# A conformer block with recorded instruction order: the limits that choose the order, from 18 phases to 49 segments

## The chip, the cores and the metric

The kernel runs on one core of a Trainium2 chip. The metric is the device time of one execution in microseconds (us); most executions of one kernel agree within 0.3%. Each run also lists the mean clock that TensorE was granted (1.00 is full speed). Engines are named as in the profile: PE is TensorE (PEld its weight loads), ACT is ScalarE, DVE is VectorE, POOL is GpSimd, SP is SyncE.

## The reference

A conformer block in bf16: B = 2 sequences of T = 4000 rows, D = 144, K = 5 taps, H = 4 heads of 36.

```python
x = x + 0.5 * (silu(layernorm(x) @ w_ff1a) @ w_ff1b)
q, k, v = heads(layernorm(x) @ w_qkv)                     # 4 heads of 36
x = x + (softmax(q @ k.T * 36**-0.5) @ v) @ w_o
a, b = split(layernorm(x) @ w_pw1)
h = a * sigmoid(b)
x = x + silu(depthwise_conv(h, dw, taps=5)) @ w_pw2
x = x + 0.5 * (silu(layernorm(x) @ w_ff2a) @ w_ff2b)
return layernorm(x)
```

The large part is attention: 2 x 4 x 4000 x 4000 exponentials.

## The kernel before

The queries are cut into 16 chunks of 500 (8 for each sequence), the keys into 63 key tiles of 64 (the last is short). One *tile* of work is 64 keys by one query chunk by 4 heads: 1008 tiles in all. A tile's scores are four 64-row matrix products into two banks of PSUM (the memory that takes TensorE's results). Then its exponentials are made either by ScalarE (one instruction over two neighbouring banks, 1000 columns) or by VectorE (seven instructions over two single banks, an approximation). Then TensorE multiplies them by the values. Everything else (feed-forward, projections, gated convolution, norms) is "background" that runs beside the attention. Six banks serve scores and background alike.

No engine decides anything at run time. While the program is built, every instruction goes through a recorder that keeps a planned clock for each engine, and the order in which they are recorded is the order in which each engine executes:

```python
def op(self, eng, name, *a, r=(), w=(), q=None, cost=0.1, kind=None, lat=None, **k):
    ...
    start = ready = self.free[eng]
    for d, raw in o.deps:
        if d.eng != eng or d.q is not None or (raw and eng != "pe"):
            ready = max(ready, d.done + self.SEM[eng])
    ...
    if eng == "pe":
        if kind != self.kind:
            start += self.SWITCH          # planned cost of another tiling mode
        self.kind = kind
    self.free[eng] = o.t1 = start + cost
```

What comes next is chosen among candidates by planned start, under limits that depend on how far attention is (`now("NAME")`). MAXQ, for one, is how many score tiles may wait for ScalarE, LIVE how many VectorE tiles may be under way, AHEAD how early ScalarE's next scores must be planned:

```python
BASE = dict(AHEAD=0.56, DSLACK=0.4, DGAP=4.0, OFREE=1, OBATCH=1, LATE=0.3, BMIN=1.6, SOON=2, LIVE=3, MAXQ=3, EARLY=2)
POLICY = {                                # one value for each of 18 phases
    "DSLACK": [0.4, 0.4, 1.5, 1.5, 1.5, 1.5, 1.5, 0.6, 1.0, ...],
    "LIVE": [3, 2, 2, 2, 3, 3, 3, 3, 3, 2, 2, 3, 3, 3, 2, 3, 3, 3],
    ...
}
def now(k):
    return POLICY[k][its[min(n_s[0], NIT - 1)][0]] if k in POLICY else BASE[k]

# in pick_any: S = scores of a tile, O = value products, T = background
near = [q for q in pe if q[0] <= pemin + PW]
deadline = act_end() - now("AHEAD")       # ScalarE must have its next scores by then
if ts is not None:
    limit = max(deadline, ts) + (now("LATE") if lag() else 0.0)
ok = [q for q in bg if max(q[0], R.free["pe"]) + q[2].req.dur + ... <= limit]
...
if ok:
    return min(ok, key=lambda q: not q[2].req.hold)      # background that fits
if s:
    return s[0]                                          # else scores
if o:
    return o[0]

def due():                                # give the next tile to VectorE?
    if n >= NIT or not DVE_EXP or live_dve[0] >= now("LIVE") or early[0] >= now("EARLY") or lag():
        return False
    return (... and R.free["dve"] < R.free["pe"] + now("DSLACK") and R.free["pe"] > last_dve[0] + now("DGAP"))
```

A ScalarE tile needs a free *pair* of banks, a VectorE tile and most background one bank at a time:

```python
def emit_S(n):
    ...
    lo, hi = banks.take_pair()            # two neighbouring banks
    scores(n, 0, lo, 0.0525)
    scores(n, 1, hi, 0.0525)
```

The softmax here doesn't subtract the row's maximum and nothing guards it: scores larger than these inputs give would overflow.

## Time and profile before

| | before |
|---|---|
| time, median of 3 runs | 938.69 us (938.61 to 938.76) |
| span of the profile, clock | 937.0 us, 0.999 |
| ScalarE busy | 893.2 us (95%), so 43.8 us idle |
| VectorE busy | 864.1 us (92%) |
| TensorE busy | 891.4 us (95%) |
| ScalarE idle: until the first exponential / to the end of the first gap / to the copy that follows the last exponential / from there on | 9.5 / 5.4 / 16.3 / 12.6 us |

Three engines stand at 92 to 95%, so busy shares alone do not name the bound. All recorded instructions carry one source line (L169, the recorder's), so groups are told apart by the names of their tiles: QT,KT is a score product, PT,VA a value product, XT,WA and WB,HT feed-forward, WQKV a value projection, PT<-PS on ScalarE an exponential, TH a tanh.

### The profile page before, as it was taken

How to read it: one execution, taken by the hardware profiler on the slowest of the kernel's cores; microseconds unless marked ns; L12 is line 12 of the kernel's file. 1: busy time of each engine (PE TensorE's matmuls, PEld its weight loads, DVE VectorE, ACT ScalarE, POOL GpSimd, SP SyncE). 2: the span in 40 equal slices, each digit the busy share in tenths (PEclk: the TensorE clock that was granted, in tenths of full speed). 3: DMA queues.
4: the chain of work that ended last, by engine and by line, in shares of the span. 5: the costliest groups of instructions: out<-in, count | busy, mean ns of one | idle time of the engine just before them, and what ended most of it. 6: DMA issues, size and time to landing. Idle time of an engine off the chain costs nothing.

```text
span 937.0 us, 26616 instructions
## 1 busy us (share of the span) xinstructions
PE 891.4 (95%) x11427; PEld 405.4 (43%) x11427; DVE 864.1 (92%) x1905; ACT 893.2 (95%) x1141; POOL 291.9 (31%) x518
## 2 busy tenths in 40 slices
PE   8999999999999999999999999999999999999996
PEld 7543434343444443344434343334344343434456
DVE  7998898999999799998989999998999899998796
ACT  5799999999999999998999999999999999999985
POOL 4120152232240551324404236203334313424233
PEclk9999999999999999999999999999999999999999
DMA  4000000000000000000000000000000000000000
GB/s 117 27 2 2 1 2 1 1 2 2 2 1 1 3 2 1 2 2 8 2 2 8 1 14 3 1 1 14 1 2 8 8 2 9 8 2 8 1 8 26
DMA packets 7319, 7.30 MB, mean 8 GB/s; under 512 B 2376, under 2 KB 7202, under 8 KB 7202
## 3 DMA queue, kind: packets, MB, share of 16 engines
q1 hardware_dynamic: 5788, 5.00, 1.8%
q8 instruction: 89, 1.46, 0.7%
q10 hardware_dynamic: 1414, 0.62, 0.3%
q14 instruction: 28, 0.23, 0.1%
HBM read 3.31 MB, written 2.30 MB: 6 GB/s over the span
## 4 chain that ended last, share of the span: by engine, by line
ACT 50%; PE 32%; DVE 14%; POOL 2%; issue 1%; DMA 0%; POOLq 0%; DVEq 0%
ACT PT L169 44%; PE PS L169 32%; DVE PT L169 8%; ACT TH L169 5%; DVE ST L169 1%; DVE HT L169 1%; POOL XN L169 1%; DVE X L169 1%; POOL RS L169 1%; DVE XT L169 1%; DVE OTF L169 1%; DMA X<-in_x_dram 0%; DVE AN L169 0%; DVE KT L169 0%; DVE XN L169 0%
## 5 line engine op out<-in xcount | busy, mean ns | idle before, releaser
L169 ACT ACTIVATE PT<-PS 128x1000 bf16<-128x1000 f32 (+1 forms) x867 | 801.7, 1046 | 13.8 <-PE PS L169 12.4
L169 PE MATMUL PS<-QT,KT 64*64 64x500 bf16 x3968 | 412.9, 384 | 27.4 <-ACT PT L169 21.6
L169 PE MATMUL PS<-PT,VA 64*37 64x500 bf16 x3968 | 361.6, 375 | 2.9 <-DVE OTF L169 1.4
L169 PEld LDWEIGHTS PS<-QT,KT 64*64 64x64 bf16 x3968 | 125.0, 104 | 225.4 <-ACT PT L169 142.4
L169 DVE TENSOR_SCALAR PT<-PS 128x500 uint16<-128x500 f32 x282 | 188.8, 671 | 11.9 <-PE PS L169 11.2
L169 DVE TENSOR_TENSOR PT<-PT 128x1000 uint16<-128x1000 uint16 (+1 forms) x282 | 190.1, 679 | 1.7
L169 POOL TENSOR_SCALAR RS<-ST 125x4 f32<-125x4 f32 x112 | 37.3, 333 | 460.2 <-DVE ST L169 455.1
L169 DVE TENSOR_SCALAR PT<-PT 128x1000 uint16<-128x1000 uint16 (+1 forms) x423 | 169.9, 418 | 2.3
L169 PEld LDWEIGHTS PS<-PT,VA 64*37 64x37 bf16 x3968 | 114.9, 95 | 113.0 <-issue 32.7
L169 POOL TENSOR_SCALAR XN<-X,RS 125x144 bf16<-125x144 bf16 x224 | 135.3, 616 | 5.8
L169 POOL TENSOR_TENSOR RS<-RS,NHALF 125x4 f32<-125x4 f32 (+2 forms) x101 | 97.8, 973 | 100.8 <-DVE RS L169 96.1
L169 ACT ACTIVATE TH<-PS 128x500 bf16<-128x500 f32 (+2 forms) x203 | 108.7, 558 | 7.1 <-PE PS L169 6.4
L169 DVE SCALAR_TENSOR_TENSOR HT<-TH,PS 128x500 bf16<-128x500 bf16 (+1 forms) x140 | 83.8, 615 | 9.7 <-ACT TH L169 9.2
L169 PE MATMUL PS<-XT,WA 72*128 72x500 bf16 (+2 forms) x280 | 73.9, 360 | 0.6 <-DVE VA L169 0.3
L169 DVE SCALAR_TENSOR_TENSOR X<-PS,X 125x288 bf16<-125x288 f32 (+1 forms) x128 | 57.2, 452 | 11.5 <-PE PS L169 9.6
L169 DVE BATCH_NORM_STATS2 ST<-X 125x6 f32<-125x288 bf16 x160 | 65.6, 447 | 1.4 <-DMA X<-in_x_dram 1.3
L169 PE MATMUL PS<-WB,HT 128*125 128x144 bf16 (+1 forms) x640 | 52.2, 230 | 1.5 <-ACT HT L169 1.1
L169 PEld LDWEIGHTS PS<-WB,HT 128*125 128x125 bf16 (+1 forms) x640 | 44.2, 136 | 15.6 <-issue 7.0
L169 PE MATMUL PS<-IDENT,XN 125*72 125x125 bf16 x512 | 42.4, 221 | 3.1 <-POOL XN L169 1.6
L169 DVE COPY XT<-PS 72x1000 bf16<-72x1000 bf16 (+1 forms) x64 | 39.6, 619 | 4.9 <-PE PS L169 4.3
L169 POOL COPY U<-U 128x2 bf16<-128x2 bf16 (+1 forms) x54 | 18.5, 368 | 73.8 <-DVE U L169 73.8
L169 PEld LDWEIGHTS PS<-IDENT,XN 125*72 125x72 bf16 x512 | 31.4, 112 | 22.1 <-issue 10.5
(88 smaller groups left out, 602.3 us busy)
## 6 DMA issues: line engine op xcount, KB each, us to landing
X<-in_x_dram SPq DMA_DIRECT2D x16, 140.6 KB
out_dram<-XN SPq DMA_DIRECT2D x14, 140.6 KB
WA<-in_w_ff1a_dram ACTq DMA_DIRECT2D x1, 144.0 KB
WB<-in_w_ff1b_dram ACTq DMA_DIRECT2D x1, 144.0 KB, 2.7
WA<-in_w_ff2a_dram SPq DMA_DIRECT2D x1, 144.0 KB
WB<-in_w_ff2b_dram SPq DMA_DIRECT2D x1, 144.0 KB
out_dram<-XN SPq DMA_DIRECT2D x2, 70.3 KB
WQKV<-in_w_qkv_dram ACTq DMA_DIRECT2D x1, 121.5 KB
```

Of the source, the lines that this page charges most:

```text
L169: ins = getattr(eng, o.name)(*o.a, **o.k)
```

## The change

Nothing is computed otherwise. A beam search over the limits, judged by the planned idle time of ScalarE and VectorE, gave a new table with a set of values for every 21 tiles. Three limits that were constants (PW, TWIN, BGPICK) come into the table, BGPICK with its old value 0 throughout, and AHEAD is tabled too. The core of the diff (twelve more lists of 49 values cut):

```diff
-    BASE = dict(AHEAD=0.56, DSLACK=0.4, DGAP=4.0, OFREE=1, OBATCH=1, LATE=0.3, BMIN=1.6, SOON=2, LIVE=3, MAXQ=3, EARLY=2)
+    SEG = 21
     POLICY = {
-        "LIVE": [3, 2, 2, 2, 3, 3, 3, 3, 3, 2, 2, 3, 3, 3, 2, 3, 3, 3],
-        "MAXQ": [3, 3, 3, 3, 3, 3, 3, 3, 2, 2, 2, 2, 2, 3, 3, 3, 3, 3],
         ...
+        "LIVE": (
+            3, 3, 2, 2, 1, 3, 3, 2, 3, 2, 3, 3, 3, 3, 3, 3,
+            2, 3, 3, 3, 3, 1, 1, 2, 2, 2, 2, 2, 2, 2, 1, 3,
+            3, 3, 3, 3, 3, 3, 2, 3, 3, 3, 3, 3, 3, 3, 3, 3,
+            3,
+        ),
+        "MAXQ": (
+            1, 1, 3, 3, 1, 3, 3, 3, 3, 3, 3, 3, 2, 2, 1, 3,
+            3, 3, 2, 2, 2, 1, 1, 2, 2, 2, 2, 2, 1, 1, 2, 2,
+            2, 2, 3, 3, 3, 2, 2, 3, 3, 3, 1, 3, 2, 2, 3, 3,
+            3,
+        ),
         ...
     }
-    BGPICK = 0
-    TWIN = 0.1
@@
     def now(k):
-        return POLICY[k][its[min(n_s[0], NIT - 1)][0]] if k in POLICY else BASE[k]
+        return POLICY[k][seg[0]]
+    seg = [0]
@@
-    PW = 0.12
-        near = [q for q in pe if q[0] <= pemin + PW]
+        near = [q for q in pe if q[0] <= pemin + now("PW")]
@@
     while n_s[0] < NIT or eq or pend or live_dve[0]:
+        seg[0] = max(seg[0], n_s[0] // SEG)
```

## The prediction

> **What bounds the kernel now.** I read the page's head first, then busy time by stretch, then the timelines of ScalarE and TensorE where ScalarE stood still. The head leaves three engines as candidates:
>
> ```profile
> span 937.0 us, 26616 instructions
> ...
> PE 891.4 (95%) x11427; PEld 405.4 (43%) x11427; DVE 864.1 (92%) x1905; ACT 893.2 (95%) x1141; POOL 291.9 (31%) x518
> ...
> ACT PT L169 44%; PE PS L169 32%; DVE PT L169 8%; ACT TH L169 5%; DVE ST L169 1%; DVE HT L169 1%; POOL XN L169 1%; DVE X L169 1%; POOL RS L169 1%; DVE XT L169 1%; DVE OTF L169 1%; DMA X<-in_x_dram 0%; DVE AN L169 0%; DVE KT L169 0%; DVE XN L169 0%
> ```
>
> The last line is the chain that ended last: half of it is ScalarE's exponentials (PT) and tanh (TH), a third TensorE. Then busy time by stretch, cut where ScalarE starts its first exponential (20.6), stops (29.3), resumes (47.6) and does the last one (905.6). After the length come busy us of PE, PEld, DVE, ACT and POOL:
>
> ```profile
> 0.00:20.60 20.60, 18.47 (x241) 16.20 (x241) 15.72 (x61) 11.08 (x23) 10.55 (x27) 1.00 0.44 116
> 20.60:29.30 8.70, 8.14 (x80) 3.16 (x77) 8.44 (x27) 8.63 (x12) 2.73 (x4) 1.00 0.32 111
> 29.30:47.60 18.30, 17.75 (x190) 10.98 (x189) 16.76 (x41) 12.96 (x28) 2.06 (x3) 1.00 0.01 2
> 47.60:450.00 402.40, 388.86 (x5110) 169.05 (x5106) 373.95 (x818) 389.74 (x477) 118.51 (x212) 1.00 0.01 2
> 450.00:850.00 400.00, 380.72 (x4864) 161.23 (x4860) 379.07 (x785) 398.19 (x494) 128.60 (x221) 1.00 0.02 5
> 850.00:905.60 55.60, 53.63 (x652) 23.20 (x649) 46.83 (x99) 53.81 (x71) 19.27 (x34) 1.00 0.01 4
> 905.60:937.00 31.40, 23.82 (x314) 21.55 (x312) 23.30 (x81) 18.84 (x41) 10.22 (x17) 0.97 0.08 24
> ```
>
> ScalarE's idle time by stretch (length less busy) is 9.5, 0.1, 5.3, 12.7, 1.8, 1.8 and 12.6 us, 43.8 in all. From 450 to 850 it is 99.5% busy: there ScalarE alone is the bound. What an order can win lies before 450, in the first gap and in the two ends. The waits say that ScalarE stands for TensorE's results, not for buffers:
>
> ```profile
> ACT PT L169 <- PE PS L169: 12.4, 20, 2.5
> ACT TH L169 <- PE PS L169: 6.4, 8, 1.3
> ```
>
> The largest such hole, first ScalarE's timeline, then TensorE's:
>
> ```profile
> 427.28 2.38 ACT L169 ACTIVATE PT<-PS 128x1000 bf16<-128x1000 f32 x3
> 431.00 0.27 ACT L169 ACTIVATE TH<-PS 80x125 bf16<-80x125 f32 x1 [1.34 <-PE PS L169]
> ...
> 428.52 0.40 PE L169 MATMUL PS<-QT,KT 64*64 64x500 bf16 x2
> ...
> 431.66 0.84 PE L169 MATMUL PS<-WB,HT 128*125 128x144 bf16 x10
> 432.43 0.71 PE L169 MATMUL PS<-WQKV,XTQ 72*64 72x72 bf16 x32
> 433.07 0.40 PE L169 MATMUL PS<-PT,VA 64*37 64x500 bf16 x4
> 433.29 0.59 PE L169 MATMUL PS<-QT,KT 64*64 64x500 bf16 x8
> ```
>
> TensorE is busy all along, but with feed-forward and projection work: from 428 to 433.29 its score products (QT,KT) come two at a time, which are VectorE's tiles; four in a row into two neighbouring banks are ScalarE's. The work is there; its order starves ScalarE.
>
> **What the Trainium skill says.** "Perfetto Trace Analysis", section "Optimization Strategy", advises to look for the gaps on the engine one optimizes and for the instruction that ends each; the reading above does that. "ScalarE: Activation LUTs", section "What ACT_TABLE_LOAD costs", gives 186 ns + 0.833 ns per element for an ACTIVATE with immediate operands and 93 ns of overlap between neighbours: 926 ns for 1000 elements. The trace is a little better: 15 exponentials from 410.99 last 13.86 us, so (13.86 - 1.05)/14 = 0.915 with a short wait inside, and undisturbed runs (4.48 us for 5 in the chain) give 0.893. "TensorEngine Tiling (Array Packing)", section "Key Properties", says that changing the tiling mode drains TensorE. The trace agrees: after four 64-row products the next 64-row group starts 0.21 to 0.23 us later, a full-array group 0.31 to 0.33, so a change costs about 0.1.
>
> **The change, part by part.** Nothing is computed otherwise. The limits by which the recorder picks the next instruction now change every 21 key tiles (49 sets) instead of by 18 phases. I built both and compared each engine's order.
>
> *Work.* Of 1008 attention tiles ScalarE does 855 + 16 short ones (before 851 + 16), VectorE 137 (141). A VectorE tile costs, by the starts of successive rows, 2 x 0.59 from PSUM + 3 x 0.33 + 2 x 0.59 = 3.35 us, so VectorE loses 13.4 us of work; ScalarE gains 4 x 0.893 = 3.6. The tail (after the last exponential) takes over some post-attention feed-forward: 4 tanh of 500 columns (0.48 each) and one of 250 (0.26) fewer, 4 Silu of 500 (0.43) and 2 of 250 (0.26) more. With a few copies and normalizations fewer (-1.7 together) ScalarE's sum is 3.6 - 2.2 + 2.2 - 1.7 = +1.9 us: 895.1 busy. TensorE's products are the same but for warm-up fillers (177 to 155) and halves in the tail; its tiling changes between first and last score rise from 1084 to 1103, 19 x 0.1 = 1.9 us on an engine with slack.
>
> *Order, steady part.* I walked TensorE's order in both, pricing each product by the trace (64-row 0.0525, 500 columns 0.21, 144 columns 0.0625, tiling change 0.1), and took the distance between successive ScalarE score tiles. Both walks are 754 us from first to last score, so TensorE is not relieved. But a distance beyond two exponentials (1.8 us) is a likely hole, and these fall from 18 to 15, their excess from 12.9 to 7.2 us; beyond 2.1 us from 8.7 to 3.7. The longest, 6.2 us, is the hole shown above; after, the longest is 4.0 there. Before 16.3 us of idle was seen from 47.6 to 905.6, against 12.9 of excess: the measure is of the right size. Scaling by 7.2/12.9 gives 9.1; I keep 9.8, since some holes are VectorE's or GpSimd's. **-6.5 us.**
>
> *Order, first gap.* In the same walk the pause between the seventh and the eighth exponential falls from 18.1 to 14.2 us, since less feed-forward of later chunks stands before chunk 1's keys: on ScalarE 4 tanh of 500 fewer, on VectorE 5 products of 500 and one of 250 (about 4 us in sum). Some of that only moves later; ScalarE's idle there should go from 5.3 to 3.1. **-2.2 us.** Until the first exponential both orders have the same instruction counts: 9.5 stays.
>
> *Tail.* ScalarE does 45 instructions instead of 41 there, TensorE 27 real products more and 22 fillers fewer. The chain through the last chunk is the same, so I let the tail grow 0.7 us while its ScalarE work grows 1.3: idle 12.0.
>
> *Sum.* Idle 9.5 + 0.1 + 3.1 + 9.8 + 12.0 = 34.5; span 895.1 + 34.5 = 929.6, and the timed run is 1.7 above the span (938.7 against 937.0): 931.3. I say 931.5.
>
> **Rivals.** *The plan does not hold.* The order was chosen by planned times; the chip's GpSimd rows vary (four XN took 4.73 us at 419.22 and 1.79 at 426.46), and a fixed order cannot react. Then new holes open where old ones closed: 936 to 940. For it: the before order was searched by a similar plan and still has 16 us of holes. Against: its largest hole is visible in the order alone, so it was planned, not a surprise. *TensorE becomes the bound.* It is 95% busy and in many 5 us slices 100%; if so, removing ScalarE holes gives nothing and the 19 tiling changes cost: 937 to 941. Against: TensorE's walk is 754 us in an 885 us stretch. *The work split wins more.* The search also counted VectorE's idle; ScalarE's and VectorE's work sums to 11 us less, and if all holes before 450 go, the time is about 921 to 925. Against: 450 to 850 has no idle to win, and VectorE doing four tiles fewer lengthens ScalarE.
>
> **Range and chances.** The first rival at half strength gives 937.5, the third at half 925.5: that is the range. Faster by over 2% needs 919.9 or less, an idle sum near 23, which is the two ends alone: 3%. Slower by over 2% would need 18.8 us of new holes: 1%.
>
> **What will show it.** ScalarE busy near 895 and idle near 34; the first gap ending near 44 instead of 47.6; the hole at the end of the seventh query chunk (1.34 + 2.46 us above) down to under 2; idle before 450 down by about 6 and unchanged after; VectorE busy near 850; the tail within 1 us of 31.4. It is wrong if ScalarE's waits for TensorE do not fall, or if the tail or the waits for VectorE grow by as much.

## The result, and the profile after

| | before | after |
|---|---|---|
| time, median (lowest to highest), 4 runs each | 938.65 us (938.58 to 938.76) | 931.46 us (931.38 to 931.59) |
| span, clock of the profiled run | 937.0 us, 0.999 | 929.6 us, 0.999 |
| ratio after to before | | 0.9923, 95% interval 0.9906 to 0.9941 |

Ratios here and below are the mean time of one kernel's runs over that of the other's of the same rounds, so not quite the ratio of the medians quoted. Executions over 1.5% slower than the fastest of the same kernel are left out of the means. The time fell by 7.2 us (0.8%).

The head of the page after, busy times and the chain of waits:

```profile
span 929.6 us, 26576 instructions
...
PE 886.9 (95%) x11413; PEld 405.4 (44%) x11413; DVE 849.9 (91%) x1880; ACT 895.0 (96%) x1142; POOL 306.1 (33%) x520
...
ACT PT L169 41%; PE PS L169 36%; DVE PT L169 8%; ACT TH L169 5%; DVE ST L169 2%; DVE HT L169 1%; DVE X L169 1%; DVE QT L169 1%; DVE OTF L169 1%; POOL RS L169 0%; DMA X<-in_x_dram 0%; DVE DG L169 0%; POOL XN L169 0%; DVE XN L169 0%; DVE XT L169 0%
```

ScalarE is busy 1.7 us *longer* in a span 7.4 us shorter; VectorE lost 14.2 us of work. Next, busy time by stretch, cut at the same events as before (first exponential, end of the seventh, the eighth, 450, 850, end of attention). The last cut, 905.6 before and 897.02 after, is where ScalarE starts the copy that follows its last exponential, which itself ended 0.9 us sooner (904.66 and 896.08). After the length come busy us of PE, PEld, DVE, ACT and POOL, each with its count, then the granted clock:

```profile
0.00:20.30 20.30, 18.42 (x238) 16.39 (x239) 15.73 (x61) 11.08 (x23) 10.55 (x27) 1.00 0.46 124
20.30:29.00 8.70, 7.95 (x81) 3.26 (x80) 7.34 (x22) 8.52 (x12) 2.09 (x3) 1.00 0.28 96
29.00:44.35 15.35, 13.88 (x150) 8.34 (x148) 13.69 (x38) 11.38 (x23) 3.50 (x5) 1.00 0.01 2
44.35:450.00 405.65, 392.61 (x5152) 169.78 (x5154) 367.89 (x798) 399.51 (x489) 122.47 (x208) 1.00 0.01 2
450.00:850.00 400.00, 382.58 (x4897) 164.65 (x4886) 377.26 (x783) 398.56 (x499) 136.03 (x225) 1.00 0.02 5
850.00:897.02 47.02, 45.60 (x592) 20.39 (x592) 42.45 (x91) 45.76 (x57) 20.82 (x38) 1.00 0.03 8
897.02:929.60 32.58, 25.87 (x319) 22.60 (x318) 25.50 (x90) 20.17 (x45) 10.60 (x15) 0.98 0.07 19
```

ScalarE's idle time, length less busy, beside that of before (same events; 450 and 850 are clock times, not events):

| stretch | before | after | change |
|---|---|---|---|
| until the first exponential | 9.52 | 9.22 | -0.30 |
| to the eighth exponential (the first gap) | 5.41 | 4.15 | -1.26 |
| to 450 | 12.66 | 6.14 | -6.52 |
| 450 to the end of attention | 3.60 | 2.70 | -0.90 |
| after attention | 12.56 | 12.41 | -0.15 |
| sum | 43.75 | 34.62 | -9.13 |

Idle fell by 9.1, busy rose by 1.7, so the span fell by 7.4. That is the whole account, and most of it lies before 450. ScalarE's waits after:

```profile
ACT PT L169 <- PE PS L169: 5.2, 16, 0.5
ACT TH L169 <- PE PS L169: 4.3, 8, 1.4
```

In the first line, exponentials waiting for scores: 12.4 us in 20 waits became 5.2 us in 16, and the longest 0.5 us instead of 2.5. The place of the former largest hole, the end of the seventh query chunk, on ScalarE and then on TensorE:

```profile
422.23 1.06 ACT L169 ACTIVATE TH<-PS 128x500 bf16<-128x500 f32 x2
423.83 1.00 ACT L169 ACTIVATE PT<-PS 128x1000 bf16<-128x1000 f32 x1 [0.54 <-PE PS L169]
```

```profile
419.28 0.41 PE L169 MATMUL PS<-QT,KT 64*64 64x500 bf16 x4
...
421.26 0.40 PE L169 MATMUL PS<-QT,KT 64*64 64x500 bf16 x2
...
421.60 1.02 PE L169 MATMUL PS<-XT,WA 72*128 72x500 bf16 x4
...
423.40 0.38 PE L169 MATMUL PS<-QT,KT 64*64 64x500 bf16 x4
```

The score groups of four (a ScalarE tile) are still about 4 us apart here, but the two tanh instructions of the feed-forward that TensorE did in between fall into that pause, and only 0.54 us of idle time is left of the former 1.34 + 2.46. The six banks are not what was short. The two recorded orders, built again from the two kernels (a reading of the programs, no run on the chip), have pairs of banks free during nearly all of both stretches. What keeps ScalarE's scores back there is this rule of the recorder, the same in both kernels:

```python
def s_start():                            # may the next score tile be a candidate?
    ...
    if b == 0 and ph > 0 and not o_done(ph - 1) and len(pend) > 3:
        return None                       # first sequence: value products of the chunk before are open
```

At the end of a chunk of the first sequence (of half a chunk, for the first two) the next chunk's scores are no candidate while more than three tiles wait for their value products; and while no score is a candidate, the limit on background is off (`limit = 1e9`), so that ready background goes before the value products that would end the state, unless buffers for exponentials run short. At the seventh chunk this lasted 4.7 us of planned time before and 2.1 after. Over the whole run it lasted half a microsecond or longer eight times before (16.9 us planned) and once after. The traces fit: of ScalarE's pauses over 0.15 us between 47 us and the end of attention (14.0 us before, 5.8 after), 8.6 us before and 1.8 after lie between 1 us before and 8 us after the ends of chunks 2 to 8. No run changed this rule alone, so that it is the cause of most of the gain is a reading and not shown.

### The profile page after: what moved, and what is told of

It is laid out like the page before. It is cut to its first block, busy times and chain, and to the rows that moved or that the text cites. A ratio compares the mean times of both kernels' runs of the same rounds, so it can differ in the third digit from the quotient of the medians.

```text
span 929.6 us, 26576 instructions
## 1 busy us (share of the span) xinstructions
PE 886.9 (95%) x11413; PEld 405.4 (44%) x11413; DVE 849.9 (91%) x1880; ACT 895.0 (96%) x1142; POOL 306.1 (33%) x520
## 4 chain that ended last, share of the span: by engine, by line
ACT 47%; PE 36%; DVE 14%; issue 1%; POOL 1%; DMA 0%; POOLq 0%; DVEq 0%
ACT PT L169 41%; PE PS L169 36%; DVE PT L169 8%; ACT TH L169 5%; DVE ST L169 2%; DVE HT L169 1%; DVE X L169 1%; DVE QT L169 1%; DVE OTF L169 1%; POOL RS L169 0%; DMA X<-in_x_dram 0%; DVE DG L169 0%; POOL XN L169 0%; DVE XN L169 0%; DVE XT L169 0%
## 5 line engine op out<-in xcount | busy, mean ns | idle before, releaser
L169 PE MATMUL PS<-QT,KT 64*64 64x500 bf16 x3968 | 413.9, 385 | 20.3 <-ACT PT L169 14.2
L169 PE MATMUL PS<-PT,VA 64*37 64x500 bf16 x3968 | 353.4, 374 | 4.9 <-DVE OTF L169 2.2
L169 POOL TENSOR_SCALAR RS<-ST 125x4 f32<-125x4 f32 x112 | 41.6, 371 | 467.2 <-DVE ST L169 462.5
L169 DVE TENSOR_SCALAR PT<-PS 128x500 uint16<-128x500 f32 x274 | 183.0, 669 | 12.8 <-PE PS L169 11.5
L169 DVE TENSOR_TENSOR PT<-PT 128x1000 uint16<-128x1000 uint16 (+1 forms) x274 | 184.0, 676 | 1.5
L169 DVE TENSOR_SCALAR PT<-PT 128x1000 uint16<-128x1000 uint16 (+1 forms) x411 | 163.8, 415 | 2.3
L169 POOL TENSOR_SCALAR XN<-X,RS 125x144 bf16<-125x144 bf16 x224 | 149.9, 680 | 5.8
L169 POOL TENSOR_TENSOR RS<-RS,NHALF 125x4 f32<-125x4 f32 (+1 forms) x103 | 100.5, 980 | 112.5 <-DVE RS L169 107.8
L169 ACT ACTIVATE TH<-PS 128x500 bf16<-128x500 f32 (+2 forms) x198 | 104.3, 549 | 5.0 <-PE PS L169 4.3
L169 DVE SCALAR_TENSOR_TENSOR X<-PS,X 125x288 bf16<-125x288 f32 x128 | 57.0, 451 | 15.3 <-PE PS L169 13.6
L169 PEld LDWEIGHTS PS<-IDENT,XN 125*72 125x72 bf16 x512 | 31.5, 112 | 21.0 <-issue 10.6
L169 PE MATMUL PS<-U,DG 128*128 128x250 bf16 (+5 forms) x204 | 34.3, 265 | 0.6 <-DVE PT L169 0.4
```

The source lines that it names most:

```text
L169: ins = getattr(eng, o.name)(*o.a, **o.k)
```

## The experiments

Twelve kernels ran, in three jobs on three chips, each job with its own runs of the kernel before (medians 939.11, 938.96 and 938.85 us). Two theories stood against each other at the start. **Order**: the gain is that ScalarE waits less for scores, because of the order alone. **Work**: the gain is VectorE's lost 14 us of work. Later a third question came up: whether the gain is *local* (each segment's limits improve their own segment) or belongs to the order as one whole.

### Adding work: d_act, d_pe, d_dve

Each takes the order after and, without changing it, doubles some instructions with their results thrown away or rewritten identically, spread over tiles 80 to 980. The repeats carry the same waits as the originals.

```diff
+    some = {...}          # 21 / 47 / 17 tiles, evenly spread
+    R.twice("E", some.__contains__, lambda a: (JUNK[:, :], a[1][:, 0, :]) + a[2:])        # d_act: 21 exponentials of 500 columns
+    R.twice("S", some.__contains__, None)                                                # d_pe: 188 score products
+    R.twice("V", some.__contains__, lambda a: (JUNK[:, :].bitcast(U16), a[1]) + a[2:])   # d_dve: 17 PSUM reads of 500 columns
```

> The changed kernel, its order untouched, with 21 extra exponentials of 128x500 on ScalarE (each a copy of half a following exponential, written to an unused tile), spread evenly over the attention: 21 x 0.48 = 10.1 us of added ScalarE work, nothing else. My theory (ScalarE is the bound wherever it has no hole, TensorE and VectorE have slack): the time rises by most of it, 7.5 to 10 us, to 939 to 941.5 from 931.5, since only a few of the 21 fall into the remaining 8.8 us of holes. Rival 'TensorE is the bound': under 4 us. Rival 'VectorE's share decides': under 4 us.

> The changed kernel, its order untouched, with the four score products of 47 ScalarE tiles issued twice (same data into the same bank): 188 x 0.0525 = 9.9 us of added TensorE work, spread evenly. My theory: TensorE's walk is 754 us in a stretch of 877, so most is absorbed: 931.5 + 0 to 3 us. Rival 'TensorE is the bound' (its page says 95% busy): 7 to 10 us more, 938.5 to 941.5.

> The changed kernel, its order untouched, with 17 extra 128x500 reads of PSUM on VectorE (copies of the first step of 17 VectorE tiles, to an unused tile): 17 x 0.59 = 10 us of added VectorE work, spread evenly. My theory: VectorE has 80 us of idle time (929.6 less 849.9), so 931.5 + 0 to 3.5 us. Rival 'VectorE's share decides' (the gain came from giving it 13 us less work): 7 to 10 us more.

| | busy added (trace) | median us | ratio to before | over after (931.9 on this chip, by 0.9923) |
|---|---|---|---|---|
| d_act | ScalarE +9.5 | 940.51 (940.40 without the run at 0.985) | 1.0040 [0.9991, 1.0088] | +8.5 |
| d_pe | TensorE +7.5 | 937.19 | 0.9986 [0.9970, 1.0003] | +5.3 |
| d_dve | VectorE +9.6 | 942.49 (three runs) | 1.0034 [1.0017, 1.0050] | +10.6 |

The kernel after itself did not run on this chip, so its 931.9 is worked out. d_act's ratio includes one run of 950.29 us at clock 0.985; the other three are 940.2 to 940.6. One run of d_dve (955.68 us, clock 0.983) is slow and not in its ratio; its fast runs scatter from 941.05 to 943.42. ScalarE behaves as the bound that it was taken for: 9.5 us of work cost 8.5. But TensorE's added work costs more than half of itself, and VectorE's, at 91% busy, about as much as itself (9.2 us in the fastest run, at clock 0.999). I had expected 0 to 3 and 0 to 3.5 us there: those expectations were wrong. The waits of ScalarE's exponentials for TensorE in d_dve:

```profile
ACT PT L189 <- PE PS L189: 11.3, 29, 2.1
```

11.3 us against 5.2 after: VectorE's delay reaches ScalarE by way of TensorE, which does its instructions in a fixed order and waits there for VectorE's tiles (8.0 us in 22 waits, after 3.3 in 10). Not all of d_dve's cost came that way. Exponential by exponential, the profiled run is 7.2 us behind the kernel after at 801 us, and 4.2 us more come at one place, where TensorE waited for GpSimd's normalized rows and the clock then fell to half:

```profile
829.00 0.63 PE L189 MATMUL PS<-IDENT,XN 125*72 125x125 bf16 x8 [2.23 <-POOL XN L189]
```

```profile
826.32:829.73 3.41, 1.18 (x20) 0.62 (x16) 1.46 (x5) 1.67 (x2) 3.02 (x9) 1.00 0.00 0
829.73:833.15 3.42, 3.42 (x30) 0.81 (x22) 3.21 (x7) 2.01 (x2) 0.00 (x0) 0.50 0.02 5
```

Idle time on VectorE is not slack in a fixed order.

### Taking work away: l_dve, l_act, l_pe

The same in the other direction, on the order *before*, and wrong in result: the squaring step is left out of 23 VectorE tiles; 24 exponentials are done for half their columns; 188 value products are left out.

```diff
+    R.without(set(ops of tag "V" in 23 tiles))                     # l_dve
+    o.a = (o.a[0][:, 0, :], o.a[1][:, 0, :]) + o.a[2:]             # l_act, in 24 tiles
+    R.without(set(ops of tag "O" in 47 tiles))                     # l_pe
```

> The kernel BEFORE, its order untouched, without one of VectorE's steps (the squaring, 128x1000 TENSOR_TENSOR) in 23 of its 141 tiles: 23 x 0.59 = 13.6 us of VectorE work less, as much as the change took from VectorE; results wrong on purpose. In the three runs with added work VectorE's 10 us cost 10.6, so VectorE's work is not free in a fixed order. Rival 'the work split won' (the change helps because VectorE has 13 us less to do): the time falls by 7 us or more, to 932 or below. Theory 'the order won' (ScalarE's stalls are set by what TensorE does when, and taking work away in a fixed order leaves most of them): it falls by 0 to 4 us, to 935 to 939.

> The kernel BEFORE, its order untouched, with 24 of ScalarE's 851 long exponentials cut to their first 500 columns: 24 x (0.893 - 0.48) = 9.9 us of ScalarE work less; results wrong on purpose. If ScalarE is the bound outside its stalls: 5 to 8.5 us less, 930 to 934. If the three engines are tied so closely that no one of them alone is the bound: 2 to 5 us less.

> The kernel BEFORE, its order untouched, without four value products (PT,VA) at 47 places: 188 x 0.0525 = 9.9 us of TensorE work less; results wrong on purpose. If the stalls of ScalarE are TensorE's lateness spread over the run: 3 to 6 us less (the added 9.9 us cost 5.2). If they are a few bursts of other work in front of a score tile, which 47 evenly spread places miss: 0 to 2.5 us less.

| | busy removed (trace) | median us (before: 938.96) | ratio to before |
|---|---|---|---|
| l_dve | VectorE -10.8 | 937.33 | 0.9981 [0.9966, 0.9996] |
| l_act | ScalarE -6.0 | 937.22 | 0.9978 [0.9964, 0.9993] |
| l_pe | TensorE -6.3 | 938.55 | 0.9994 [0.9979, 1.0009] |

The page's busy line of l_dve:

```profile
PE 890.9 (95%) x11427; PEld 405.4 (43%) x11427; DVE 853.3 (91%) x1882; ACT 892.5 (95%) x1141; POOL 287.5 (31%) x518
```

VectorE has about the busy time here (853.3) that it has after the change (849.9), and the time is 1.6 us lower, not 7.2. So the *Work* theory falls as the main cause: in the old order, three quarters of the busy time (10.8 of 14.2 us) are worth about a quarter of the gain, and 3.2 us at the far end of the interval. The work removed is more than the busy time removed (13.6, 9.9 and 9.9 us by the expectations), because the records of neighbouring instructions overlap: an exponential is shown 1.00 us long, and in a row they start 0.884 us apart (median). Together with the first three kernels this is a one-sided picture: 7.5 to 9.6 us added to any one engine cost 5 to 11 us, 6 to 11 us taken from any one gives 0.4 to 1.7. But work was added to the order after and taken from the order before, so the one-sidedness is not shown within one order.

### One set of limits for all tiles: o_const

The kernel after with every limit at the constant that BASE had (all 1009 entries alike), so that neither search had any say.

```diff
+        "DSLACK": ((1009, 0.4),),  "LIVE": ((1009, 3),),  "MAXQ": ((1009, 3),),  ...
```

> The same program with one constant set of limits (the defaults) instead of any table: another order, 141 VectorE tiles like before. A test of the reading by TensorE's order alone: distances between ScalarE score tiles beyond 1.8 us sum to 9.7 us of excess (before 12.9, changed 7.2), ScalarE's work by counts is 1.4 us less than before, the first gap is as before. If that walk is all that matters: steady idle 12.1 (16.3 before, 8.8 changed), time about 932.5 to 934. Rival: holes that the walk does not show (ScalarE waiting for a free exponential tile or bank, a longer tail) count as much, and limits tuned over the whole run matter: 938 to 943. Rival 'work split': as before, 938 to 939.

942.59 us, ratio to before 1.0034 [1.0017, 1.0051]. VectorE has 141 tiles, as many as before. Exponentials waited 16.2 us for scores (before 12.4, after 5.2). Varying the limits along the way is worth 3.5 us in the old table and 11 us in the new. There is a warning in this run for the prediction's method: in TensorE's order of o_const the excess of the distances between ScalarE's score tiles is 9.7 us, *less* than before's 12.9, and yet it is slower. The walk saw the right thing in the pair before/after and is no general ruler.

### Half and half: o_first and o_630

The limits after for the first part, those before for the rest: o_first to tile 503 (the first sequence), o_630 to tile 629.

```diff
+    limits(n) = after(n) if n < 504 else before(n)      # o_first
+    limits(n) = after(n) if n < 630 else before(n)      # o_630
```

> The limits of the changed kernel for the first batch (tiles 0 to 503), those of the kernel before for the second: the order is that of the changed kernel up to there, then a new one. VectorE does 133 tiles (141 before, 137 changed). Rival 'the work split won' (fewer VectorE tiles, faster): 931.5 or less. Theory 'the order won, and it is one plan through to the end': the first batch gains as in the changed kernel (score tiles' end of the first batch about 7 us earlier than before), ScalarE's work rises 5.5 us over the changed kernel's, and the tail is longer (TensorE's tail has 386 products, 101 of them fillers, against 320 and 36): 937 to 943.

> The limits after for tiles 0 to 629 (all of the first batch and two chunks more), the limits before for the rest. Theory 'the gain is local': the first gap and the holes before 450 us, where nearly all of the gain lay, are as after: 931 to 933 us. Theory 'one plan': planned end 924.2, 1.0 under before and 4.3 over after: 935 to 938 us, with the loss late, after 600 us.

o_first: 948.06 us, ratio 1.0098 [1.0080, 1.0116], the slowest but with the *fewest* VectorE tiles (133), which does not fit the Work theory either. Its attention does end 1.8 us sooner than before's (last exponential at 902.9 instead of 904.7), but what follows takes 41.7 us instead of 32.3. Busy time by stretch around the end of o_first, columns as above, the granted clock third from last:

```profile
898.00:904.00 6.00, 3.36 (x32) 0.82 (x28) 5.59 (x13) 2.91 (x5) 5.33 (x8) 0.90 0.03 8
904.00:909.00 5.00, 4.66 (x23) 3.75 (x24) 2.44 (x8) 1.83 (x4) 3.95 (x11) 0.50 0.07 23
909.00:944.60 35.60, 27.60 (x365) 24.56 (x362) 21.38 (x73) 19.75 (x47) 8.94 (x12) 0.93 0.06 17
```

Two losses show. TensorE has 3.36 us of work in 6.00 us (it waits for the last tiles), and its clock then falls to 0.50 for 6.83 us (902.74 to 909.57). And the tail is longer by plan: 36.5 us after the last exponential, before 28.6, after 30.9. Its 387 products (before 324) are not left-over background alone: by the recorded orders they are 286 products and 101 fillers, before 262 and 58, after 293 and 36 (the expectation above puts before's products beside after's fillers). Fillers stand where TensorE is planned to wait, so against the order after it is waiting that grew. That both losses come from a table fitted to another backlog is my reading; no run separates them.

o_630: 936.13 us, ratio 0.9975 [0.9963, 0.9987], inside the 935 to 938 us of the theory that the order is one whole, outside the 931 to 933 us of the local one. At the end of chunk 9 it leads before by 6.7 us (after leads by 7.5); at the end of chunk 12 it is 0.1 behind, at the last chunk 0.1 ahead. A lead at a chunk's end is not yet time won, since background may have been put off: the kernel after also falls, to 1.7 at chunk 12, but is back at 8.4 at the last chunk. So the loss against it lies after chunk 12, under the other table's limits; some 2 us of it belong to the profiled run alone, the slowest of the five (938.07, the others 936.02 to 936.63), whose clock was at half from 817.47 to 820.89.

### Only the place of the largest hole: o_hole

The limits before everywhere, but those after for tiles 378 to 461, the seventh query chunk and the start of the next, where the largest hole had been closed.

```diff
+    limits(n) = after(n) if 378 <= n < 462 else before(n)
```

> The limits before everywhere but for tiles 378 to 461 (the seventh query chunk and the start of the next), which take the limits after. Theory 'the gain is local' (a hole is closed where the new limits hold, the rest stays): the hole at the end of the seventh chunk, 1.34 + 2.46 us, shrinks to about 0.5, so 935 to 936 us. Theory 'the order is one plan to the end' (limits fitted to one course of the work do harm after another): the recorder's own planned end is 932.0 against 925.2 for before, so about 7 us slower than before, 944 to 947 us, with a longer part after the last exponential (TensorE's order holds 29.6 us of products after the last score, before 25.5).

946.01 us, ratio 1.0074 [1.0061, 1.0087]: slower by 7 us, as the theory of one whole had it. The hole itself, on ScalarE in o_hole:

```profile
430.09 0.28 ACT L169 ACTIVATE TH<-PS 80x125 bf16<-80x125 f32 x1 [1.80 <-PE PS L169]
432.82 1.00 ACT L169 ACTIVATE PT<-PS 128x1000 bf16<-128x1000 f32 x1 [2.45 <-PE PS L169]
```

It is still there, 1.80 + 2.45 us, with the very limits in force that go with 0.54 us in the order after. So these limits do not close the hole; the state in which the work arrives there (what background is ready, how many tiles wait for their value products) does, and that state is made earlier. In o_hole's recorded order the rule of `s_start` held the scores back for 5.8 us of planned time there, longer than before. Later o_hole loses more: against before it stands at +2.2 us after chunk 8, +5.7 after chunk 10 and +3.4 after chunk 16, and its tail is 35.7 us instead of 32.3.

### A longer search, and the kernel after once more: s_best, after_again

s_best starts from the table after and changes single values by annealing, judged by the recorder's planned end alone; 280 of its 686 values differ. after_again is the kernel after, as the yardstick of that job.

```diff
     POLICY = {
-        (after's 14 lists of 49)
+        (14 lists of 49, planned end 919.0 instead of 919.9)
```

> A further search from the limits after, by planned end alone (919.0 against 919.9 after). If the plan ranks orders even at 1 us: 929.5 to 931, ratio to after 0.9975 to 0.9995. If the plan is only good to a few us: anywhere from 929 to 936. TensorE's walk gives 7.8 us of excess against 7.2 after, so that measure says no gain.

> The changed kernel itself, as the yardstick of this job. Both theories: 0.992 to 0.993 of the kernel before, 931 to 932 us.

s_best: 932.56 us, ratio to before 0.9934 [0.9922, 0.9946]; after_again: 931.68 us. The further 0.9 us of plan came out as 0.9 us of loss: at that size the plan ranks no more. No version found here beats the kernel after.

after_again gave something unlooked for. Five of its six runs took 931.60 to 931.89 us, the sixth, the profiled one, 942.64 us at a mean clock of 0.986 (its ratio of 0.9943 has that run in it; the medians give 931.68 / 938.85 = 0.9924). Its trace shows where: stretches of that run, then the same stretches of the kernel after in its first, undisturbed profile:

```profile
36.00:42.00 6.00, 5.04 (x34) 3.02 (x32) 5.78 (x15) 4.13 (x10) 0.70 (x1) 0.81 0.00 1
42.00:62.00 20.00, 20.00 (x166) 8.21 (x168) 11.66 (x37) 13.07 (x17) 4.96 (x7) 0.50 0.00 1
```

```profile
36.00:42.00 6.00, 5.04 (x67) 3.01 (x66) 5.94 (x16) 4.99 (x11) 0.69 (x1) 1.00 0.01 1
42.00:62.00 20.00, 19.41 (x265) 9.30 (x267) 17.57 (x57) 19.15 (x25) 6.39 (x10) 1.00 0.01 2
```

The same order, the same 5.04 us of busy TensorE in the first gap, and in one execution the clock drops to half for about 24 us (from the mean clocks 0.63 of 39 to 42 and 0.69 of 60 to 66 it was at 0.50 from 39.8 to 63.7): 166 products instead of 265 from 42 to 62. The end of the first query chunk comes at 147.63 instead of 137.53 us, and this lag of 10 us stays to the end, where it is 11.3. Before, the same 6 us have 5.67 us of TensorE work. That the order after runs nearer to a fall of the clock is not shown by this: in the 3.41 us before the fall TensorE was busy for 2.46 us, in the undisturbed profile of the same order for 2.45 at the same place, and in the kernel before for 2.27 from 865.40 on, where nothing fell. 1 of the 10 executions of after had such a fall and none of the 29 of before, which is too few to tell them apart. d_act (950.29 us, clock 0.985) and d_dve (955.68 us, clock 0.983), which share this first gap, each had one such run of four; those have no trace, so that their cause is the same is not shown.

Nor do falls need this gap or this table. Four more traces have one, each of 3.41 us, each just after TensorE had waited for GpSimd's normalized rows: d_dve (at 829.73, wait 2.23 us, shown above), o_const (817.92, 1.28), o_hole (825.71, 1.98) and o_630 (817.47, 0.97). In the 3.41 us before them TensorE was busy for 1.18 to 2.08 us. They make part of the scatter of these kernels' runs.

### What the orders say together

The recorder's planned end (its own arithmetic, no measurement), the excess by the prediction's walk along TensorE's order, and the chip:

| order | planned end | walk's excess | VectorE tiles | measured median |
|---|---|---|---|---|
| s_best | 919.0 | 7.8 | 137 | 932.6 |
| after | 919.9 | 7.2 | 137 | 931.5, 931.7 |
| o_630 | 924.2 | 7.0 | 135 | 936.1 |
| before | 925.2 | 12.9 | 141 | 938.7 to 939.1 |
| o_const | 929.1 | 9.7 | 141 | 942.6 |
| o_first | 931.2 | 6.4 | 133 | 948.1 (clock 0.990 to 0.994) |
| o_hole | 932.0 | 12.8 | 139 | 946.0 |

The measured time is 11.6 to 14 us above the planned end, in nearly the same order; o_first, which lost clock, is 17 above. Neither the walk's excess nor the number of VectorE tiles ranks them. The time for which the rule of `s_start` held scores back does not rank them either (2.9 us planned in all in after, s_best, o_630 and o_first; o_const 14.8, before 18.1, o_hole 20.1): it tells of the first sequence only.

## Why the prediction was right

The predicted 931.5 us met 931.46. Its mechanism, that ScalarE starved by TensorE's order and not for buffers, held, and the free pairs of banks agree with it. By its own steps:

- **Work.** Right: ScalarE busy 895.0 (said 895.1), VectorE 849.9 (said near 850).
- **Steady part, -6.5 us.** Right in place and mechanism: idle from the eighth exponential to the end of attention fell from 16.3 to 8.8, so by 7.4 us, of which 6.5 lie before 450; the hole at the seventh chunk went from 3.8 to 0.5 us, said under 2. The waits named in advance (exponentials for scores) fell by 7.2 us. The method behind the number deserves less credit than the number: o_const and o_first have less excess than before by the same walk and are slower.
- **First gap, -2.2 us.** Mis-sized: ScalarE resumed at 44.35, as said, but its idle in the gap fell by 1.3 us (5.41 to 4.15): the stretch from the seventh to the eighth exponential became 2.95 us shorter, but 1.58 us of that was ScalarE's busy time (12.96 to 11.38), which only moved elsewhere.
- **450 to 850, "ScalarE alone is the bound".** Too strong: between 434 and 825 us d_pe, with work added to TensorE alone, falls behind the kernel after by 3.3 us more (from 2.6 to 5.9).
- **Head, no change.** It gave 0.3 us.
- **Tail, +0.7 us.** Mis-sized: the stretch after attention grew by 1.2 us (31.4 to 32.6), just outside the "within 1 us" named as a test; its idle was 12.4 and not 12.0.
- **Sum.** Idle 34.6 against 34.5 said. The errors (+0.9 in the gap, -0.3 in the head, +0.4 in the tail, -1.0 from the eighth exponential on) cancel; the agreement to 0.1 us is partly luck. In the range, the upper end does not follow from its rival: half the way to 936 to 940 is about 934 to 936, not 937.5. And the 926 ns taken from the Trainium skill's formula are an estimate; the exponentials in a row start 0.884 us apart (median).

The rivals. *The plan does not hold*: fell for this order; GpSimd's rows did get longer (XN 680 ns mean against 616, busy 306 us against 292), but no new hole opened. In four of the other orders it shows, as the waits of 0.97 to 2.23 us for such rows. What the plan could not know is the clock that fell in one run of ten. *TensorE becomes the bound*: fell, as the time is 931.46 and not 937 to 941, and in the old order 6.3 us less of TensorE's busy time give 0.4 us; but the argument used against it, that TensorE has slack, is wrong in its plain form, as 7.5 us more cost 5.3 us. *The work split wins more*: fell, as the time is not 921 to 925; l_dve gave 1.6 us, and o_first, with the fewest VectorE tiles, was the slowest.

What stays open: that the state at the seventh chunk is made before tile 378 is shown by o_hole; which earlier choice makes it is not, nor was the rule of `s_start` varied on the chip. And the finer segments were not tried without the newly tabled limits (AHEAD, PW, TWIN), so what each of the two is worth is not known.

## What to carry to other kernels

Where one engine is near full and its waits name another that is itself busy, look at the order in which the busy one does its work: a few microseconds of misplaced background can starve the first, and no engine's work needs to shrink to cure it. In a fixed order, idle time is not slack, and work removed is not time won: 7.5 to 9.6 us of work added to the new order cost 5 to 11 us, 6 to 11 us removed from the old one gave under 2. When an engine starves, look also for the rule of the scheduler that kept its work back, before blaming buffers. Search results of this kind hold as a whole: a table's half, or its one good place, put into another table cost 7 to 9 us or gave most of the gain back; and run such a kernel often enough, and look at the clock of each trace, to see whether the clock falls in some of its executions.

## What the Trainium skill lacked or had wrong

- "TensorE: Matmul & The Clock Gate", section "A second HAM failure mode: psum-queue depth-cycling", says that frequent short idles of TensorE can make its clock gate swing; the runs agree in so far as the clock fell without a long idle, and the page has no measure for how much idling it takes. In after_again the clock fell to 0.50 at 39.77 us though no wait of TensorE in the trace from 28 to that point is longer than 0.50 us, with 2.46 of the last 3.41 us busy by the records; with the same order it did not fall in nine other executions. In o_first it fell at 902.74 us after waits of at most 0.67 us, 1.71 of 3.41 us busy, and did not fall after 839.00, with 1.43 of 3.41 us busy.
- The same page, section "What's actually happening", has the full clock back after one busy window of about 3.4 us. Four traces agree (half clock for 3.41 us in d_dve, o_const, o_630 and o_hole); in o_first it took 6.83 us, and in after_again 23.89 us (39.77 to 63.66), with TensorE shown busy for all of the 20 us from 42 to 62.
- "Perfetto Trace Analysis", section "Identifying the Most-Contended Engine", takes occupancy as the measure of the bound and has one optimize the engine where it is highest. Here an engine with a lower share (VectorE, 91%) passed on about all of 9.6 us of added work (+10.6 us, part of it with a fall of the clock), and 6.0 us less work on ScalarE (95%) gave only 1.7 us. The page has nothing on recorded, fixed orders, in which engines are coupled both ways.
